# Key and query rows of the first attention stage put in unused weight places, and its transfers in one fixed order

## The chip, the cores and the metric

The kernel runs on one core of one Trainium2 chip. The metric is the device time of one execution in microseconds (us); the quoted time is the median of repeated runs. The engines are TensorE (PE; its weight loads are shown as PEld), VectorE (DVE), ScalarE (ACT), GpSimd (POOL) and SyncE (SP), which here only issues transfers (DMA) between the chip's main memory and its on-chip memory. Each engine works through its instructions in order.

## The reference

Causal attention with a bias that depends on running sums, for 4 batches of 8 heads with 576 tokens and 64 values each, followed by two dense blocks with 2304 tokens, width 512 and inner width 2048.

```python
def _attn_ref(q, k, v, s):
    scores = scale * np.matmul(q, k.transpose(0, 1, 3, 2))
    cum = np.cumsum(np.maximum(s, 0.0), axis=-1)
    bias = -(cum[:, :, :, None] - cum[:, :, None, :])
    scores = np.where(causal, -1000000000.0, scores + np.minimum(bias, 0.0))
    scores = scores - np.max(scores, axis=-1, keepdims=True)
    attn = np.exp(scores)
    attn = attn / (np.sum(attn, axis=-1, keepdims=True) + 1e-09)
    return np.matmul(attn, v)

# x is attn_out with the heads side by side: 2304 x 512
h = x @ w_in
g = np.maximum(h, 0.0) + alpha * np.minimum(h, 0.0)
x = g @ w_out
h = x @ w_in2
y = (h * np.clip(h + 3.0, 0.0, 6.0) / 6.0) @ w_out2
```

The weights arrive as 64-bit floats; the kernel turns them into 32-bit ones on the chip.

## The kernel before

Tokens are taken in two groups for the attention: the first 256 of each batch (stage one), then the other 320. Stage one goes by pairs of heads (`Pair`): batch 0 is pairs 0 to 3, batch 1 pairs 4 to 7, batch 2 pairs 8 to 11. `attention0` first handles pairs 0 to 7, then, in a second call, pairs 8 to 11, while the first dense layer (`moe1`) already runs over the 512 tokens of batches 0 and 1.

One head of a pair passes PE (scores, line 322), DVE (maximum, line 328), ACT (exponential, line 333), DVE (sum and reciprocal, lines 334 and 335), POOL (scaling, line 337), PE (transposition, line 593), ACT or DVE (copy `pT`, lines 595 and 597); the pair's values follow on PE (line 603), ACT (`xhi`, line 611) and DVE (`xlo`, line 612). The running sums of `s` are made once (`cumulate`), written to `cum_scratch` in main memory, and read back as four extra rows beside the keys and queries, two of them data and two constants, so that one matmul adds the bias. Pairs 0 and 1 do without: their biases come from extra matmuls with `pick` and `cum2`. For all others the tile `kr` holds four places (`Rows.n = 4`), and pair i uses place i mod 4. So pair 6 waits for place 2 until pair 2's scores are done, pair 7 for pair 3, and pairs 8 to 11 for pairs 4 to 7. Values (`vraw`, one tile for two pairs) have three buffers.

The weights of the first layer come in 8 units (`load_unit`) of four tiles of 512 KB, each of which has a place of its own in on-chip memory (`wi60`, `wo71` and so on: matrix, unit, part). A unit is read raw, then turned into two 32-bit halves by `split_part`: ACT (lines 142 and 160, sometimes 150), POOL (lines 144 and 147), DVE (lines 152, 155, 161). `moe1` goes through 16 slices f of the inner width, two per unit: 12 matmuls into `h` (line 248), ACT (line 697), DVE with `beta` (line 698), ACT (line 701), DVE (line 702), and 12 matmuls into `y` (line 675), two slices behind. `beta` is made by DVE from `alpha_sb` (line 307), whose transfer is issued in `cumulate`.

A planner in the framework lays out each engine's order of instructions from its own estimate of when each is ready; earlier lines of the program come first among those that are ready, and conversions of weights stand back behind the attention in stage one. Instructions marked `pin` or `keep_in_program_order` stay in the order of the program. All transfers named here are issued by SP. The order on SP before is: `s`, pairs 0 to 3, sums out, rows for pairs 2 to 5, pairs 4 and 5, units 0 and 1, `alpha`; then pair 6 with its rows and pair 7 with its rows when their places are free, units 2 and 3, the keys of pairs 8 to 11 with their rows, units 4 to 7 with the values of pairs 8 to 11 among them.

Of the kernel before, what the change touches and what calls it, by code (L numbers as in the profile page):

```python
# [9 lines left out]
F32 = mybir.dt.float32  # L10
# [5 lines left out]
P = 128  # L16
# [8 lines left out]
WB0 = 6  # L25
WB = 4

W_LD = (9, 11)
W_AT = (5, 11)

A2_AT = 4
# [30 lines left out]
def attention_moe_moe(ctx, tc, qt, kt, kq2, kqs, vs4, vp, s, w_in1, w_out1, alpha, w_in2, w_out2, out):  # L62

    nc = tc.nc
# [217 lines left out]
    def cumulate(pool, pairs):  # L282

        pin = tc.keep_in_program_order
        cum2, pick, zero = pool.cum2, pool.pick, pool.zero
        s_sb = pool.tile([BH, S], F32, tag="wcv", bufs=WB0, name="s_sb")
        pin(nc.sync.dma_start(s_sb, s))
        for pr in pairs[:4]:
            pr.load(pool, pin)
        nc.vector.tensor_scalar(s_sb, s_sb, 0.0, 8.0, op0=ALU.max, op1=ALU.mult)  # L290
        cum = pool.tile([BH, S], F32, tag="wcv", bufs=WB0, name="cum")
        nc.vector.tensor_tensor_scan(cum, s_sb, zero[:BH].to_broadcast([BH, S]), initial=0.0, op0=ALU.add, op1=ALU.add)
        for c0, c1, copies in ((0, NA, 2), (NA, S, 1)):
            cols = slice(c0, c1)
            for j in range(copies):
                high = cum2[j * D : j * D + BH, cols]
                pin(nc.scalar.activation(high, cum[:, cols], AF.Copy))
                pin(nc.vector.tensor_tensor(cum2[j * D + BH : (j + 1) * D, cols], cum[:, cols], cum2[:BH, cols].bitcast(F32), op=ALU.subtract))
            pin(nc.sync.dma_start(cum_d[:, :, cols].rearrange("t b s -> (t b) s"), cum2[:D, cols].bitcast(F32)))
            if c0 == 0:  # L300
                pool.rows.load(2, 2, pin)
                pool.rows.load(4, 2, pin)
        for pr in pairs[4:6]:
            pr.load(pool, pin)
        load_w1(2)
        pin(nc.sync.dma_start(alpha_sb, alpha))
        nc.vector.tensor_scalar(beta, alpha_sb, -1.0, 1.0, op0=ALU.mult, op1=ALU.add)

# [229 lines left out]
    class Rows:  # L538


        n = 4

        def __init__(self, pool):
            self.kq = pool.tile([P, self.n, 2, 2, NA], F32, name="kr")
            keys = self.kq[:R, :, 0].rearrange("r n j k -> r n (j k)")
            nc.scalar.activation(keys, ident[:R, None, :1].to_broadcast([R, self.n, 2 * NA]), AF.Copy, scale=0.0, bias=-1.0)
            nc.gpsimd.memset(self.kq[:R, :, 1], 1.0)

        def load(self, first, n, pin=lambda ins: ins):
            at = first % self.n  # L550
            for which in range(2):
                rows = slice(which * R // 2, (which + 1) * R // 2)
                for j in range(2):
                    src = cum_d[:, 2 * first + j : 2 * (first + n) : 2, :NA]
                    pin(nc.sync.dma_start(self.kq[rows, at : at + n, which, j], src))

    values_of = {}

    class Pair:
# [5 lines left out]
        def load(self, pool, pin=lambda ins: ins):  # L565
            i, self.pool = self.i, pool
            if i < 2:
                kq = pool.tile([P, 2, NA], F32, tag="wcv", bufs=WB0, name="kq")
                self.k, self.q = kq[:, 0], kq[:, 1]
                pin(nc.sync.dma_start(kq, kq2[i]))  # L570
            else:
                kq = pool.rows.kq[:, i % Rows.n]
                self.k, self.q = kq[:, 0], kq[:, 1]
                pin(nc.sync.dma_start(kq[R : R + D], kqs[i - 2]))
            if i % 2 == 0:
                self.load_v(pin)

        def load_v(self, pin=lambda ins: ins):
            i, pool = self.i, self.pool
            values_of[i // 2] = pool.tile([P, 4, 2, D], F32, tag="vraw", bufs=3 if i < H else 2, name="vraw")  # L580
            pin(nc.sync.dma_start(values_of[i // 2], vs4[i // 2]))

        def scores(self, j):
# [30 lines left out]
    def attention0(pool, pairs, lag):  # L614
# [15 lines left out]
        def ahead(to):  # L630
            nonlocal loaded
            while loaded <= min(to, len(pairs) - 1):
                if pairs[0].i == 0:
                    pairs[loaded].load(pool, tc.keep_in_program_order)
                    pool.rows.load(loaded, 1, tc.keep_in_program_order)
                else:
                    pairs[loaded].load(pool)
                loaded += 1

        if pairs[0].i == 0:  # L640
            keep_clock(pool.busy, 18)
            cumulate(pool, pairs)
            loaded = 6
        else:
            pool.rows.load(H, H // 2)
        ahead(1)
        for i, pr in enumerate(pairs):
            for j in range(2):
                waiting.append((pr, j, pr.scores(j)))
                if j == 1:  # L650
                    ahead(i + (Rows.n if pairs[0].i == 0 else 2))
                if len(waiting) > lag:
                    finish()
                yield
# [78 lines left out]
    def attend(att, upto, pool=None):  # L733

        nonlocal done
        while done < upto:
            done += 1
            next(att, None)
            if pool is not None and done in W_LD:
                load_w1(len(units) + 1)  # L740
            if pool is not None and done in W_AT:
                more_w(pool)

# [345 lines left out]
```

## Time and profile before

| what | value |
|---|---|
| median of 3 runs | 1001.95 us (1001.57 to 1003.31) |
| time of the profiled execution | 1001.04 us |
| its span, first to last instruction | 999.3 us, so 1.74 us lie around it |
| mean granted TensorE clock | 0.989 of full speed |
| PE busy | 972.0 us, 97% |
| DVE busy | 614.2 us, 61% |
| ACT busy | 633.0 us, 63% |
| POOL busy | 439.4 us, 44% |

The shares are means over the whole span. The change touches what happens in the first tenth of it, so the table says little on it, and stretches of that tenth have to be read for themselves.

### The profile page before, as it was taken

The page shows a single profiled execution, that of the slowest core. Times are in us where ns is not written, and L with a number is a line of the kernel's source. Part 1 is how long each engine was busy: PE and PEld are TensorE (multiplying, and loading weights), DVE is VectorE, ACT ScalarE, POOL GpSimd, SP SyncE. Part 2 cuts the span into 40 slices and gives each one's busy share as a digit, 9 for nine tenths or more (in the row PEclk, how much of TensorE's full clock was granted, in tenths as well). Part 3 has the DMA queues.
Part 4 walks back from the last instruction along what each step waited for, and adds up shares of the span by engine and source line. Part 5 has one row for each costly group of instructions (what it writes and reads, how often), then busy time and mean ns, then how long its engine had stood idle before and what let it go on. Part 6 is the DMA issues. An engine that isn't in the chain of part 4 may idle for free.

```text
span 999.3 us, 18072 instructions
## 1 busy us (share of the span) xinstructions
PE 972.0 (97%) x6218; PEld 873.5 (87%) x6218; DVE 614.2 (61%) x1502; ACT 633.0 (63%) x1434; POOL 439.4 (44%) x587
## 2 busy tenths in 40 slices
PE   8689999999999999999999999999999999999998
PEld 5468788999999998998998888999999988888886
DVE  6858884466666666666654885977658863222222
ACT  6668778678768778778855655756656743232322
POOL 6554667657666667666643763433112230000000
PEclk9879999999999999999999999999999999999999
DMA  6990014113122223122105322434248734333422
GB/s 220 298 358 1 24 31 132 41 46 91 53 76 74 61 67 98 52 67 83 52 14 177 109 91 72 191 118 144 98 169 304 257 130 151 103 127 91 162 64 85
DMA packets 59828, 114.47 MB, mean 115 GB/s; under 512 B 5704, under 2 KB 21880, under 8 KB 59736
## 3 DMA queue, kind: packets, MB, share of 16 engines
q1 hardware_dynamic: 59736, 113.32, 34.3%
q8 instruction: 49, 0.80, 0.3%
q14 instruction: 43, 0.35, 0.1%
HBM read 84.84 MB, written 28.46 MB: 113 GB/s over the span
## 4 chain that ended last, share of the span: by engine, by line
PE 93%; DMA 2%; ACT 2%; issue 1%; DVE 1%; SPq 0%; POOL 0%; ACTq 0%; DVEq 0%; POOLq 0%
PE y L675 20%; PE h L248 20%; PE o L1042 20%; PE a L879 10%; PE b L879 5%; PE s L410 4%; PE pv L472 4%; PE pt L447 4%; PE c L879 2%; PE s L322 2%; DMA vraw<-in_vs 1%; DMA kr<-cum_scratch 1%; PE h L534 1%; PE pv L603 1%; DMA wraw<-in_w_out 1%
## 5 line engine op out<-in xcount | busy, mean ns | idle before, releaser
L248 PE MATMUL h<-xhi,wi 128*128 128x256 f32 (+1 forms) x896 | 227.0, 322 | 2.8 <-DVE gt L698 1.5
L1042 PE MATMUL o<-wo,gh 128*128 128x512 f32 x576 | 173.5, 389 | 1.1 <-DVE gt L893 1.1
L248 PEld LDWEIGHTS h<-xhi,wi 128*128 128x128 f32 x896 | 156.4, 191 | 16.4 <-DVE gt L698 1.9
L675 PE MATMUL y<-gh,wo 128*128 128x256 f32 (+1 forms) x896 | 162.0, 315 | 0.0
L675 PEld LDWEIGHTS y<-gh,wo 128*128 128x128 f32 x896 | 133.8, 190 | 11.2 <-ACT gh L701 0.4
L248 PE MATMUL h<-xlo,wi 128*128 128x256 f32 (+1 forms) x448 | 143.2, 320 | 0.2 <-DVE xlo L612 0.2
L161 DVE TENSOR_TENSOR gl<-gr,gh 128x512 fp32r<-128x512 f32 (+1 forms) x80 | 51.3, 643 | 126.5 <-ACT gh L160 111.9
L1042 PEld LDWEIGHTS o<-wo,gh 128*128 128x128 f32 x576 | 107.9, 188 | 23.5 <-DVE gt L893 1.3
L160 ACT ACTIVATE gh<-gr 128x512 fp32r<-128x512 f32 (+1 forms) x80 | 46.9, 588 | 119.3 <-PE o L1042 117.7
L879 PE MATMUL a<-x,wc 128*128 128x288 f32 x768 | 112.9, 295 | 0.3 <-ACT z L886 0.3
L144 POOL TENSOR_SCALAR wcv<-wcv 128x512 f32<-128x512 f32 x64 | 47.7, 753 | 142.0 <-ACT wcv L142 139.0
L1042 PE MATMUL o<-wo,gl 128*128 128x512 f32 x288 | 108.2, 389 | 0.0
L879 PEld LDWEIGHTS a<-x,wc 128*128 128x128 f32 x768 | 106.0, 188 | 0.8 <-ACT z L886 0.5
L675 PE MATMUL y<-gl,wo 128*128 128x256 f32 (+1 forms) x448 | 91.6, 317 | 0.0
L248 PEld LDWEIGHTS h<-xlo,wi 128*128 128x128 f32 x448 | 85.6, 191 | 6.5 <-DVE xlo L612 0.7
L422 POOL TENSOR_SCALAR t<-t,rec 128x384 f32<-128x384 f32 (+2 forms) x96 | 65.4, 683 | 57.5 <-DVE rec L421 32.3
L413 DVE CUSTOM_DVE_ANT_0 t<-s,mask 128x384 f32<-128x384 f32 (+2 forms) x96 | 53.4, 563 | 53.3 <-PE pt L447 34.1
L698 DVE SCALAR_TENSOR_TENSOR gt<-gt,beta,h 128x256 f32<-128x256 f32 (+1 forms) x112 | 61.7, 552 | 32.2 <-ACT gt L697 31.0
L418 ACT ACTIVATE t<-t,m 128x384 f32<-128x384 f32 (+2 forms) x96 | 67.1, 700 | 17.0 <-DVE m L413 15.8
L675 PEld LDWEIGHTS y<-gl,wo 128*128 128x128 f32 x448 | 69.7, 190 | 6.0 <-issue 0.2
L702 POOL TENSOR_TENSOR gl<-gt,gh 128x256 fp32r<-128x256 f32 x80 | 59.1, 740 | 29.3 <-ACT gh L701 27.4
L701 ACT ACTIVATE gh<-gt 128x256 fp32r<-128x256 f32 (+1 forms) x112 | 53.1, 476 | 29.3 <-DVE gt L698 27.7
(135 smaller groups left out, 2000.3 us busy)
## 6 DMA issues: line engine op xcount, KB each, us to landing
g_scratch<-gt SPq DMA_DIRECT2D x64, 288.0 KB
wraw<-in_w_in SPq DMA_DIRECT2D x32, 512.0 KB
wraw<-in_w_out SPq DMA_DIRECT2D x32, 512.0 KB
gr<-g_scratch SPq DMA_DIRECT2D x16, 1024.0 KB
kraw<-in_kt SPq DMA_DIRECT2D x32, 288.0 KB
qraw<-in_qt SPq DMA_DIRECT2D x32, 160.0 KB
vraw<-in_vp SPq DMA_DIRECT2D x32, 160.0 KB
y_scratch<-yt SPq DMA_DIRECT2D x18, 256.0 KB
```

What stands on the lines that cost most here:

```text
L144: keep(nc.gpsimd.tensor_scalar(cf, cf, W_MOST, -W_MOST, op0=ALU.min, op1=ALU.max))
L161: keep(nc.vector.tensor_tensor(lo, of, hi.bitcast(F32), op=ALU.subtract))
L248: nc.tensor.matmul(dst, lt, r, start=first and i == 0, stop=last and i == len(terms) - 1)
L413: nc.vector.tensor_tensor_reduce(t[:n, a:e], sc[:n, : e - a], mask[:n, MASK + n - (e - a) :][:, : e - a] if e == w else mask[:n, : e - a], ...
L418: nc.scalar.activation(t[:n, :w], t[:n, :w], AF.Exp, bias=m[-1][:n], scale=-1.0, accum_out=den[:n])
L422: nc.gpsimd.tensor_scalar(t[:n, :w], t[:n, :w], rec[:n], 1.0, op0=ALU.mult, op1=ALU.mult)
L675: nc.tensor.matmul(ys[dc // per][:, o : o + n], which[:, dc * P : (dc + 1) * P], gg, start=(f == 0 and which is wl and dc % per == 0), sto ...
L698: nc.vector.scalar_tensor_tensor(gt, gt, beta[:, f : f + 1], hp[:, :n], op0=ALU.mult, op1=ALU.add)
L701: nc.scalar.activation(gh, gt, AF.Copy)
L702: (nc.vector if n == 512 else nc.gpsimd).tensor_tensor(gl, gt, gh.bitcast(F32), op=ALU.subtract)
L879: nc.tensor.matmul(dst[:, :NX2], lt, r, start=first and n == 0, stop=n == len(terms) - 1, skip_group_check=not first,)
L1042: nc.tensor.matmul(op[i], lt[:, tsl], r, start=(f == 0 and r is wh and lt is gh), stop=(f == FC - 1 and lt is gl))
```

## The change

Pairs 2 to 7 get a tile each. These tiles (`Pair.fill`) lie in places of the weights' units 6 and 7, whose raw weights are now loaded only once the pairs are done. Each is filled with its constants by one ACT instruction and one POOL instruction, and gets its rows by two transfers (`load_rows`). Pairs 8 to 11 have the tile `Rows` for themselves, filled by two POOL instructions, with four transfers of keys and four of rows. Nothing of stage one waits for a place any more. The order on SP is written out in `cumulate`: `s`, pairs 0 to 3, sums out, rows of pairs 2 to 5, pairs 4 and 5, unit 0, pairs 6 and 7 with their rows, unit 1, keys and rows of pairs 8 to 11, units 2 to 5, `alpha`. The values have four buffers in place of three. The loads of units 2 and 3 after steps 9 and 11 of stage one (`W_LD`) go.

```diff
--- before.py
+++ after.py
@@ -25,7 +25,6 @@
 WB0 = 6
 WB = 4
 
-W_LD = (9, 11)
 W_AT = (5, 11)
 
 A2_AT = 4
@@ -285,6 +284,8 @@
         cum2, pick, zero = pool.cum2, pool.pick, pool.zero
         s_sb = pool.tile([BH, S], F32, tag="wcv", bufs=WB0, name="s_sb")
         pin(nc.sync.dma_start(s_sb, s))
+        for pr in pairs[2:]:
+            pr.fill()
         for pr in pairs[:4]:
             pr.load(pool, pin)
         nc.vector.tensor_scalar(s_sb, s_sb, 0.0, 8.0, op0=ALU.max, op1=ALU.mult)
@@ -298,11 +299,17 @@
                 pin(nc.vector.tensor_tensor(cum2[j * D + BH : (j + 1) * D, cols], cum[:, cols], cum2[:BH, cols].bitcast(F32), op=ALU.subtract))
             pin(nc.sync.dma_start(cum_d[:, :, cols].rearrange("t b s -> (t b) s"), cum2[:D, cols].bitcast(F32)))
             if c0 == 0:
-                pool.rows.load(2, 2, pin)
-                pool.rows.load(4, 2, pin)
+                for pr in pairs[2:6]:
+                    pr.load_rows(pin)
         for pr in pairs[4:6]:
             pr.load(pool, pin)
+        load_w1(1)
+        for pr in pairs[6:]:
+            pr.load_rows(pin)
+            pr.load(pool, pin)
         load_w1(2)
+        pool.rows.load(pin)
+        load_w1(NU - 2)
         pin(nc.sync.dma_start(alpha_sb, alpha))
         nc.vector.tensor_scalar(beta, alpha_sb, -1.0, 1.0, op0=ALU.mult, op1=ALU.add)
 
@@ -538,21 +545,18 @@
     class Rows:
 
 
-        n = 4
-
         def __init__(self, pool):
-            self.kq = pool.tile([P, self.n, 2, 2, NA], F32, name="kr")
-            keys = self.kq[:R, :, 0].rearrange("r n j k -> r n (j k)")
-            nc.scalar.activation(keys, ident[:R, None, :1].to_broadcast([R, self.n, 2 * NA]), AF.Copy, scale=0.0, bias=-1.0)
-            nc.gpsimd.memset(self.kq[:R, :, 1], 1.0)
-
-        def load(self, first, n, pin=lambda ins: ins):
-            at = first % self.n
+            self.kq = pool.tile([P, H // 2, 2, 2, NA], F32, name="kr")
+            for which in range(2):
+                nc.gpsimd.memset(self.kq[:R, :, which], 2.0 * which - 1.0)
+
+        def load(self, pin):
+            for i in range(H // 2):
+                pin(nc.sync.dma_start(self.kq[R : R + D, i], kqs[H + i - 2]))
             for which in range(2):
                 rows = slice(which * R // 2, (which + 1) * R // 2)
                 for j in range(2):
-                    src = cum_d[:, 2 * first + j : 2 * (first + n) : 2, :NA]
-                    pin(nc.sync.dma_start(self.kq[rows, at : at + n, which, j], src))
+                    pin(nc.sync.dma_start(self.kq[rows, :, which, j], cum_d[:, 2 * H + j : 3 * H : 2, :NA]))
 
     values_of = {}
 
@@ -566,18 +570,31 @@
             i, self.pool = self.i, pool
             if i < 2:
                 kq = pool.tile([P, 2, NA], F32, tag="wcv", bufs=WB0, name="kq")
-                self.k, self.q = kq[:, 0], kq[:, 1]
                 pin(nc.sync.dma_start(kq, kq2[i]))
+            elif i < H:
+                kq = self.kq
+                pin(nc.sync.dma_start(kq[R : R + D], kqs[i - 2]))
             else:
-                kq = pool.rows.kq[:, i % Rows.n]
-                self.k, self.q = kq[:, 0], kq[:, 1]
-                pin(nc.sync.dma_start(kq[R : R + D], kqs[i - 2]))
+                kq = pool.rows.kq[:, i - H]
+            self.k, self.q = kq[:, 0], kq[:, 1]
             if i % 2 == 0:
                 self.load_v(pin)
 
+        def fill(self):
+            part, nm = divmod(self.i % 4, 2)
+            self.kq = wp.tile([P, 2, 2, NA], F32, tag=f"{('wi', 'wo')[nm]}{NU - 2 + self.i // 4}{part}", name="kr")
+            keys = self.kq[:R, 0].rearrange("r j k -> r (j k)")
+            nc.scalar.activation(keys, ident[:R, :1].to_broadcast([R, 2 * NA]), AF.Copy, scale=0.0, bias=-1.0)
+            nc.gpsimd.memset(self.kq[:R, 1], 1.0)
+
+        def load_rows(self, pin):
+            for which in range(2):
+                rows = slice(which * R // 2, (which + 1) * R // 2)
+                pin(nc.sync.dma_start(self.kq[rows, which], cum_d[:, 2 * self.i : 2 * self.i + 2, :NA]))
+
         def load_v(self, pin=lambda ins: ins):
             i, pool = self.i, self.pool
-            values_of[i // 2] = pool.tile([P, 4, 2, D], F32, tag="vraw", bufs=3 if i < H else 2, name="vraw")
+            values_of[i // 2] = pool.tile([P, 4, 2, D], F32, tag="vraw", bufs=4 if i < H else 2, name="vraw")
             pin(nc.sync.dma_start(values_of[i // 2], vs4[i // 2]))
 
         def scores(self, j):
@@ -630,25 +647,19 @@
         def ahead(to):
             nonlocal loaded
             while loaded <= min(to, len(pairs) - 1):
-                if pairs[0].i == 0:
-                    pairs[loaded].load(pool, tc.keep_in_program_order)
-                    pool.rows.load(loaded, 1, tc.keep_in_program_order)
-                else:
-                    pairs[loaded].load(pool)
+                pairs[loaded].load(pool)
                 loaded += 1
 
         if pairs[0].i == 0:
             keep_clock(pool.busy, 18)
             cumulate(pool, pairs)
-            loaded = 6
-        else:
-            pool.rows.load(H, H // 2)
+            loaded = len(pairs)
         ahead(1)
         for i, pr in enumerate(pairs):
             for j in range(2):
                 waiting.append((pr, j, pr.scores(j)))
                 if j == 1:
-                    ahead(i + (Rows.n if pairs[0].i == 0 else 2))
+                    ahead(i + 2)
                 if len(waiting) > lag:
                     finish()
                 yield
@@ -736,8 +747,6 @@
         while done < upto:
             done += 1
             next(att, None)
-            if pool is not None and done in W_LD:
-                load_w1(len(units) + 1)
             if pool is not None and done in W_AT:
                 more_w(pool)
```

## Rows read from the trace of the kernel before

**Rows 1.** Stretches: length; busy us (instructions) of PE, PEld, DVE, ACT, POOL; PEclk; DMA share; GB/s.

```profile
25.00:69.00 44.00, 31.06 (x161) 20.84 (x162) 32.11 (x110) 27.16 (x79) 23.99 (x43) 0.80 0.98 342
31.88:69.00 37.12, 25.93 (x122) 17.57 (x121) 25.26 (x88) 22.48 (x64) 19.63 (x34) 0.77 0.97 352
55.00:65.00 10.00, 7.08 (x40) 4.86 (x39) 7.80 (x35) 6.86 (x25) 3.94 (x8) 0.99 1.04 409
65.00:72.70 7.70, 7.70 (x28) 5.47 (x27) 5.59 (x20) 6.88 (x20) 6.94 (x13) 0.56 0.97 384
69.00:148.00 79.00, 79.00 (x362) 63.62 (x362) 66.10 (x104) 62.35 (x111) 48.66 (x65) 0.98 0.11 34
```

**Rows 2.** Chain that ended last: start us, us, what it was.

```profile
24.79 9.17 DMA vraw<-in_vs
...
35.97 6.18 DMA wraw<-in_w_out
...
42.16 8.38 DMA kr<-cum_scratch
...
50.68 1.62 PE s L322 x4
...
68.96 6.19 PE h L248 x20
```

**Rows 3.** Timeline of SP, which issues transfers: start, us, line, transfer, count.

```profile
20.34 0.33 SPq L306 DMA_DIRECT2D alpha_sb<-in_alpha  x1
...
24.79 0.33 SPq L581 DMA_DIRECT2D vraw<-in_vs  x1
...
40.96 4.00 SPq L555 DMA_DIRECT2D kr<-cum_scratch  x4
```

**Rows 4.** What SP waited for: us in total, times, longest.

```profile
SPq L555 <- DMA wraw<-in_w_out: 5.4, 4, 2.6
```

**Rows 5.** Timeline of DVE; in brackets the idle time before and its releaser.

```profile
27.16 0.68 DVE L152 SCALAR_TENSOR_TENSOR wcv<-wcv,wraw 128x512 uint32<-128x512 uint32 x1
...
31.88 0.17 DVE L307 TENSOR_SCALAR beta<-alpha_sb 128x16 f32<-128x16 f32 x1
...
35.32 0.29 DVE L328 CUSTOM_DVE_ANT_0 t<-s,mask 128x128 f32<-128x128 f32 x1 [1.88 <-PE s L322]
...
40.56 0.99 DVE L152 SCALAR_TENSOR_TENSOR wcv<-wcv,wraw 128x512 uint32<-128x512 uint32 x1
...
55.91 0.29 DVE L328 CUSTOM_DVE_ANT_0 t<-s,mask 128x128 f32<-128x128 f32 x1 [5.42 <-PE pv L603]
...
64.54 0.66 DVE L161 TENSOR_TENSOR wo<-wcv,wo 128x512 fp32r<-128x512 f32 x1
...
67.25 0.75 DVE L698 SCALAR_TENSOR_TENSOR gt<-gt,beta,h 128x512 f32<-128x512 f32 x1 [0.67 <-ACT gt L697]
```

**Rows 6.** Timeline of ACT: the first fill and the first unit's conversion.

```profile
2.02 1.91 ACT L546 ACTIVATE kr<-ident 4x2048 f32<-4x2048 f32 x1
...
20.35 0.67 ACT L142 ACTIVATE wcv<-wraw 128x512 f32<-128x512 f32 x1 [1.86 <-DMA wraw<-in_w_in]
```

**Rows 7.** Timeline of PE: the run of matmuls before the first scores.

```profile
1.45 7.00 PE L534 MATMUL h<-busy 128*128 128x512 bf16 x18 [1.45 <-DVE busy L757]
```

**Rows 8.** Timeline of POOL.

```profile
1.73 1.79 POOL L547 MEMSET kr<- 4x2048 f32 x1
...
3.96 3.48 POOL L763 TENSOR_SCALAR pick<-ident 32x32 fp32r<-32x32 f32 x8
11.83 0.83 POOL L337 TENSOR_SCALAR t<-t,rec 128x128 f32<-128x128 f32 x2 [4.39 <-DVE rec L335]
...
40.99 2.21 POOL L337 TENSOR_SCALAR t<-t,rec 128x128 f32<-128x128 f32 x2
```

**Rows 9.** Timeline of DVE: second half of unit 2 converted.

```profile
81.84 0.68 DVE L161 TENSOR_TENSOR wi<-wcv,wi 128x512 fp32r<-128x512 f32 x1
```

**Rows 10.** Timeline of PE: the matmuls that read it.

```profile
85.89 0.48 PE L248 MATMUL h<-xhi,wi 128*128 128x512 f32 x1
```

## The prediction

> **What bounds the kernel now.** I read the windows of the first 150 us, then the chain of waits through the slow part of them, then SP's timeline, to see why transfers come late, then those of DVE, ACT and POOL, to see what would be late next.
>
> The windows show where time lies open. From 69 us to 148 us PE is busy in all 79.00 us [rows 1]: whatever is gained must be gained ahead of that, and reaches the end only if PE then stays as full. In the 44 us from 25 to 69 PE is busy for 31.06 us, DVE for 32.11, ACT for 27.16 and POOL for 23.99. So PE is idle for 12.9 us and DVE for 11.9 us, and DVE is the busiest.
>
> The chain of waits says on what [rows 2]. From 24.79 to 50.68 us it runs almost wholly through transfers: the values of pair 6 (9.17 us), a tile of weights (6.18 us), the rows of pair 8 (8.38 us). Only then do the scores of pair 8 go, and at 68.96 us PE's full stretch begins with slice 2 of the first layer. The reader is to see that small loads stand in one queue with 512 KB tiles. SP gives the values of pair 6 out at 24.79 us, after `alpha` at 20.34 us and so behind all eight tiles of units 0 and 1; the rows of pair 8 go out from 40.96 us, behind units 2 and 3 [rows 3]. For the rows alone SP waited 5.4 us on earlier tiles of weights [rows 4].
>
> What does a late transfer cost? Read on DVE, which carries most work here: its timeline has two waits that end with a pair whose data were late [rows 5]. One of 1.88 us ends at 35.32 us, when pair 6's scores come. One of 5.42 us ends at 55.91 us: DVE starts on pair 8, whose buffers lie where those of pairs 0 to 7 lay and come free with pair 7's values, and those stood on PE behind pair 8's scores, which waited for the rows. Together 7.3 us. The other 4.6 us of DVE's 11.9 are short waits of the chain PE, DVE, ACT, POOL.
>
> **The change, part by part.** *Order of transfers.* Unit 0 keeps its place, and its first tile lands by 20.35 us, when ACT ends a wait for it [rows 6]. With 409 GB/s, the rate of a stretch full of weights [rows 1], a tile of 512 KB takes 1.28 us and a load of 256 KB 0.64. So I estimate: unit 0 in by 20.35 + 3 x 1.28 = 24.2; pairs 6 and 7 (three loads of 256 KB and four small ones) by about 26.5; unit 1 by 31.6; pairs 8 to 11 by 34.5; units 2 to 5 (16 tiles, 20.5 us) by 55; `alpha` by about 55.5. So pair 6 can be scored some 8 us before DVE's wait at 35.32 ended, pair 8 some 16 us before 50.68. Unit 1 comes some 5 us later by it, but it is converted behind unit 0: before, the conversion of these two units on DVE runs from 27.16 to 65.2 us [rows 5], so that costs nothing. With the data there, both waits of DVE go: **-7.3 us**. The bounds: -1.9 us if only the first of them goes, -11.9 us if all of DVE's idle time in the stretch is filled.
>
> *Fills.* ACT has six instructions of 4x512 for one of 4x2048, which took 1.91 us [rows 6]. Between a quarter of that each (no change in sum) and 0.67 us each, as for the 128x512 conversion beside it, that is 0 to 2.1 us more, at a time when PE runs its opening matmuls from 1.45 to 8.45 us [rows 7]; PE can't score before 8.45, which covers it. POOL has two of 4x2048 and six of 4x512 for one that took 1.79 us [rows 8]: by the same quarter, 2 x 1.79 + 6 x 0.45 = 6.3, so 4.5 us more. `pick`, 3.48 us from 3.96 on, is needed for the first scores; it is earlier in the program, and POOL's next work after it is at 11.83 us, so 4.4 us of idle time wait there. But the transfers of rows need the fills. I take **+0.5 us**, between 0 and +4.5 (all of it ahead of `pick`).
>
> *Row transfers.* 16 small ones in place of 20; with nobody waiting at their end: 0.
>
> *`alpha` last.* `beta` is first used at 67.25 us before [rows 5]. With the gain that is about 61 us, against 55.5 for the transfer: hidden, by some 5 us.
>
> *Weights.* Units 4 and 5 come earlier, 6 and 7 wait for pairs 6 and 7, long done by 55 us: 0. The fourth buffer of values: 0, as no row shows anything waiting for one alone.
>
> *Denser work.* The two engines disturb each other: DVE's step on line 152 took 0.68 us at 27.16 and 0.99 us at 40.56 [rows 5], and beside it two scalings on POOL took 2.21 us at 40.99, against 0.83 at 11.83 [rows 8]. Less idle time brings more of that: I take **+0.5 us**, from 0 to +3 (24 conversion steps on DVE in the stretch, first at 27.16, last at 64.54, a third of them slowed by 0.3 us on both engines).
>
> If the two excluded each other strictly, those 24 steps of 0.68 us (16.3) and POOL's 23.99 us would take 40.3 of the 44 us already: a rival, below. I don't take it for the sum, because POOL's 23.99 holds the time in which it was blocked.
>
> The Trainium skill ("SBUF — State Buffer", the section on the doors to the memory) says that a GpSimd instruction and a VectorE one with two inputs from that memory share a pair of ports as an exclusive lock, held for a whole instruction. By it the gain would stop at the rival's size; the trace agrees in kind, by the 2.21 against 0.83 us.
>
> *Clock.* From 65 to 72.7 us the granted clock is 0.56, so most of it at 1.2 GHz, while PE is busy throughout [rows 1]. At 2.4 GHz those 7.7 us would take 7.7 x 0.56 = 4.3: 3.4 us to gain, if PE is fuller before. The engines ahead of it decide, and the same mix of work comes before it: 0, with -3.4 as its bound.
>
> Sum: -7.3 + 0.5 + 0.5 = **-6.3 us**. Against the profiled execution, 999.3 + 1.74 around it = 1001.04 us, that gives 994.7. The runs' median lies 0.9 us above that execution, so I say **995.0 us**. A difference under about 0.2% (2 us) can't be told from none here.
>
> **Rivals.** *All open time is filled.* Pairs 6 to 11 in time let PE, DVE and POOL mesh: DVE's 11.9 us and the clock's 3.4 go: 15.3, about 986 us. For it speaks that no engine is busy for more than 32.11 of the 44 us; against it, that a head goes through four engines in turn, so that short waits stay. Chance 0.12.
>
> *Conversion decides.* PE's full stretch takes weights as they come: unit 2's second half is done on DVE at 81.84 + 0.68 = 82.5 us [rows 9], and the matmuls that read it start at 85.89 us [rows 10], only 3.4 us behind. If conversion, with DVE at 66.10 of 79 us, can't move up, PE waits at slice 4, and the gain is at most 3.4 us: 997.6 to 1001, middle 999. Against it: conversion of unit 1's end and unit 2 stood behind pair 8 on POOL and DVE before, and so moves with it. Chance 0.12.
>
> *DVE and POOL exclude each other.* Then the stretch can shrink from 44 to 40.3 us, by 3.7, whatever comes early: 997.3 us. For it, the stretched steps above; against it, the blocked time that is counted twice. Chance 0.06. (The rule named above says this.)
>
> *Slower: `beta` blocks DVE.* `beta` stands at 31.88 us in DVE's order [rows 5]. If the planner expects `alpha` early and leaves `beta` there, DVE stands until 55.5 us with 25.26 us of work [rows 1] behind it: it reaches the state of 69 us at 80.8, 11.8 us later, 1013 us. It decides from the point at which over 13.5 us (69 - 55.5) of that work stands behind `beta`. Against it: before, `beta` came only when `alpha` was surely there, since DVE did not idle ahead of it. Chance 0.10.
>
> **How the numbers follow.** The forecast has 0.60, with a range of its own of 991 to 998.5 from the bounds of its terms. The range runs from 988.5 to 1000.8: it leaves out most of the first rival, 0.09, all of the last, 0.10, and the edge of the conversion case, 0.01. Faster by over 0.2%: 0.60 x 0.97 + 0.12 + 0.12 x 0.35 + 0.06 x 0.8 = 0.79; slower 0.10 + 0.01 = 0.11; the rest, 0.10, is no change.
>
> **What would show it.** Right: scores of pair 6 by 27 us and of pair 8 before 48; no wait of DVE over 2 us between 30 and 60 us; the chain of waits without transfers of `vraw` and `kr` after 30 us; PE's full stretch from about 62 us and 79 us without a gap after it. Wrong: a long wait of DVE that ends with `beta`; PE waiting for `wi` around slice 4; the first scores well after 8.4 us; a second stretch at 1.2 GHz longer than 7.7 us.

## The result, and where the time went

The changed kernel takes 1010.23 us (median of 6 runs, 1008.96 to 1012.14); the kernel before takes 1002.8 us beside it. The ratio is 1.0073, with an interval of 1.0054 to 1.0091. It is slower, by some 7 us, where 995.0 us was predicted, and it lies outside the range. The profiled execution took 1009.54 us, with a span of 1007.7 us; all times below are in it.

Start where the change acts first. POOL's timeline of the changed kernel, and under it the first scores on PE (start, us, line, what, count, and in brackets the idle time before and what ended it):

```profile
1.73 3.85 POOL L551 MEMSET kr<- 4x2048 f32 x2
5.53 1.91 POOL L588 MEMSET kr<- 4x512 f32 x4
...
7.63 0.98 POOL L588 MEMSET kr<- 4x512 f32 x2
8.59 1.77 POOL L772 TENSOR_SCALAR pick<-ident 32x32 fp32r<-32x32 f32 x8
```

```profile
9.31 0.32 PE L329 MATMUL s<-cum,pick 64*128 64x128 f32 x1 [1.05 <-POOL pick L772]
```

All fills stand ahead of `pick`, which starts at 8.59 us where it started at 3.96 [rows 8]. PE, which was busy with its opening matmuls until 8.45 us [rows 7], now waits 1.05 us for it. That is about one microsecond. The next lines show what stood late behind it: ACT's timeline, and then DVE's.

```profile
21.67 0.66 ACT L141 ACTIVATE wcv<-wraw 128x512 f32<-128x512 f32 x1 [2.87 <-DMA wraw<-in_w_in]
23.03 0.66 ACT L141 ACTIVATE wcv<-wraw 128x512 f32<-128x512 f32 x1 [0.70 <-DMA wraw<-in_w_out]
```

```profile
24.97 0.19 DVE L341 TENSOR_SCALAR den<-den 128x2 f32<-128x2 f32 x1 [4.21 <-ACT t L340]
...
57.19 0.28 DVE L335 CUSTOM_DVE_ANT_0 t<-s,mask 128x128 f32<-128x128 f32 x1
...
63.17 0.57 DVE L314 TENSOR_SCALAR beta<-alpha_sb 128x16 f32<-128x16 f32 x1 [1.08 <-DMA alpha_sb<-in_alpha]
...
70.01 0.76 DVE L160 TENSOR_TENSOR wo<-wcv,wo 128x512 fp32r<-128x512 f32 x1
...
72.70 0.75 DVE L709 SCALAR_TENSOR_TENSOR gt<-gt,beta,h 128x512 f32<-128x512 f32 x1 [1.22 <-ACT gt L708]
```

The first tile of unit 0 is awaited until 21.67 us, 1.3 us later than before [rows 6], and ACT stands for it with heads behind it in its order; DVE stands 4.21 us for those. It is natural to put the late tile down to the fills, but SP's waits (us in total, times, longest) speak against it, first of the kernel before, then of the changed one:

```profile
SPq L555 <- DMA cum_scratch<-cum: 2.5, 1, 2.5
```

```profile
SPq L593 <- DMA cum_scratch<-cum: 3.7, 1, 3.7
```

SP issues unit 0 behind the rows of pairs 2 to 5, and these wait until the sums written to `cum_scratch` have landed, 2.5 us before and 3.7 now. So the first tile goes out 1.3 us later. The lines are SP's, of the kernel before, of the changed one, and of e1 and e8 below:

```profile
14.24 0.59 SPq L127 DMA_DIRECT2D wraw<-in_w_in  x1
```

```profile
15.51 0.59 SPq L126 DMA_DIRECT2D wraw<-in_w_in  x1
```

```profile
15.27 0.59 SPq L126 DMA_DIRECT2D wraw<-in_w_in  x1
```

```profile
14.43 0.59 SPq L127 DMA_DIRECT2D wraw<-in_w_in  x1
```

With `pick` ahead of the fills (e1) the tile goes out 1.0 us late as well, and with the fills ahead of `pick` in the kernel before (e8) it is only 0.2 us late. So, by these profiles of one execution each, the fills did not make this transfer late. What made the sums land later is not shown; in e10, whose edit touches only later steps, the rows went out at 10.02 us in place of 10.52.

The waits for pair 6 (1.88 us) and ahead of pair 8 (5.42 us) are gone, as predicted, but both pairs come later: pair 6 to DVE at 37.92 us, against 35.32 before, and pair 8 at 57.19, against 55.91 [rows 5]. The last step of unit 1's conversion, the end of the row of conversion steps, is at 70.01 us (64.54 before), and the first `gt` of the first layer 2.7 us behind it, as before (67.25 against 64.54): 5.45 us late.

The chain that ended last (start, us, what) shows the queue:

```profile
1.80 3.78 POOL kr L551 x2
...
17.12 9.81 DMA wraw<-in_w_out
...
30.71 10.69 DMA kr<-in_kqs
...
44.49 9.58 DMA wraw<-in_w_in
54.09 9.05 DMA alpha_sb<-in_alpha
...
73.50 5.43 PE h L247 x12
```

`vraw` and the cumulated rows have left it, but the keys of pairs 8 to 11 are in it at 30.71 us, where I had said that no `kr` would be, and transfers still fill it from 17 to 63 us, each of 9 to 11 us from its issue. The fills are in it too, in the place of PE's opening matmuls. PE's slice 2 starts at 73.50 us instead of 68.96 [rows 2].

Two of the stretches of [rows 1], and the 25 us ahead of them:

```profile
0.00:25.00 25.00, 18.80 (x98) 11.56 (x99) 10.99 (x47) 13.63 (x39) 15.49 (x39) 0.98 0.68 199
25.00:69.00 44.00, 36.09 (x177) 24.58 (x176) 34.18 (x126) 27.46 (x90) 23.30 (x44) 0.81 0.99 349
69.00:148.00 79.00, 77.82 (x348) 61.35 (x347) 64.13 (x105) 65.75 (x115) 52.06 (x68) 0.94 0.10 33
```

From 25 to 69 us PE and DVE are busier than before by 5.03 and 2.07 us: the stretch is denser, but it began with more left to do: up to 25 us DVE had been busy for 10.99 us, where it was busy for 15.46 before, and PE for 18.80 in place of 22.31. In the 79 us that were full, PE is idle for 1.18 us and the clock is at 0.94 instead of 0.98. By these two rows the clock alone takes 0.04 x 79, an estimate of some 3 us of PE's time, so it is a good part of the loss.

How much of the loss is there by the end of the first layer's blocks? SP's stores of their results, first before and then after:

```profile
161.36 0.85 SPq L686 DMA_DIRECT2D y_scratch<-yt  x2
...
225.97 0.90 SPq L686 DMA_DIRECT2D y_scratch<-yt  x2
```

```profile
166.34 0.38 SPq L697 DMA_DIRECT2D y_scratch<-yt  x1
...
233.43 0.39 SPq L697 DMA_DIRECT2D y_scratch<-yt  x1
```

5.0 us at the first block, 7.5 at the second, 8.4 in the span: more than half of it is there at the first block, and most of the rest at the second.

### The profile page after: what moved, and what is told of

It reads as the page before. It is cut to its first block, busy times and chain, and to the rows that moved or that the text cites. A ratio compares the mean times of both kernels' runs of the same rounds, so it can differ in the third digit from the quotient of the medians.

```text
span 1007.7 us, 18107 instructions
## 1 busy us (share of the span) xinstructions
PE 980.6 (97%) x6218; PEld 879.4 (87%) x6218; DVE 616.9 (61%) x1502; ACT 635.9 (63%) x1439; POOL 446.3 (44%) x594
## 4 chain that ended last, share of the span: by engine, by line
PE 88%; DMA 4%; ACT 3%; DVE 1%; SPq 1%; POOL 1%; issue 1%; ACTq 0%; DVEq 0%; POOLq 0%
PE o L1051 19%; PE y L686 19%; PE h L247 19%; PE a L888 10%; PE b L888 5%; PE s L417 4%; PE pv L479 4%; PE pt L454 4%; PE c L888 2%; DMA kr<-in_kqs 1%; DMA wraw<-in_w_out 1%; DMA wraw<-in_w_in 1%; DMA alpha_sb<-in_alpha 1%; PE s L329 1%; SPq L126 1%
## 5 line engine op out<-in xcount | busy, mean ns | idle before, releaser
L143 POOL TENSOR_SCALAR wcv<-wcv 128x512 f32<-128x512 f32 x64 | 50.7, 801 | 134.4 <-ACT wcv L141 130.6
```

The lines of the kernel that those rows point to most:

```text
L143: keep(nc.gpsimd.tensor_scalar(cf, cf, W_MOST, -W_MOST, op0=ALU.min, op1=ALU.max))
```

## The experiments

The theories at the start: A, the fills ahead of `pick` cost the start; B, `alpha` comes late; C, earlier heads of pairs 6 and 7 push the conversion of units 0 and 1 back; D, only the planner's new order. Ratios are to the kernel before, with their intervals; "first `gt`" is line 709's (698 in the kernel before) on DVE.

**e1_pick_first.** `pick` and the memsets pinned in the order in which they are written, `pick` first.

```
-    nc.gpsimd.memset(self.kq[:R, 1], 1.0)
+    tc.keep_in_program_order(nc.gpsimd.memset(self.kq[:R, 1], 1.0))
...   (the same for Rows' memsets and for pick)
```

> The changed kernel with its constant fills on POOL put behind the eight instructions that make pick. Late start (theory A: the fills ahead of pick make the first scores 0.9 us late, and the units' transfers 1.3 us late, and ACT then stands on unit 0 while heads wait): first scores back at 8.4 us, ACT's wait for unit 0 below 2 us, time down by 3 to 5 us from the changed kernel, to about 1006. Late alpha (theory B): down by at most 1 us. Early heads push the conversion of weights back (theory C): down by at most 1.5 us. Re-planning as such (theory D): a change of either sign up to 3 us.

1004.82 us, 1.0016 (1.0002 to 1.003): 0.0057 of the 0.0073 is back. The heads come early now (first scores at 7.54 us), but look at DVE's timeline:

```profile
50.90 0.29 DVE L335 CUSTOM_DVE_ANT_0 t<-s,mask 128x128 f32<-128x128 f32 x1
...
64.40 0.17 DVE L314 TENSOR_SCALAR beta<-alpha_sb 128x16 f32<-128x16 f32 x1 [3.08 <-DMA alpha_sb<-in_alpha]
...
67.96 0.85 DVE L160 TENSOR_TENSOR wo<-wcv,wo 128x512 fp32r<-128x512 f32 x1
...
70.05 0.74 DVE L709 SCALAR_TENSOR_TENSOR gt<-gt,beta,h 128x512 f32<-128x512 f32 x1
```

Pair 8 is 5.0 us earlier than before, as the forecast wanted; yet DVE then waits 3.08 us for `alpha`, unit 1's conversion ends 3.4 us later than before, and the first `gt` is 2.8 us late.

**e2_alpha_early.** The transfer of `alpha` right behind that of `s`.

```
         pin(nc.sync.dma_start(s_sb, s))
+        pin(nc.sync.dma_start(alpha_sb, alpha))
...
         load_w1(NU - 2)
-        pin(nc.sync.dma_start(alpha_sb, alpha))
```

> The changed kernel with alpha transferred right after s. Theory B (beta and so the first layer's gate wait for alpha at 63 us): DVE's beta before 20 us, the first gate before 68 us in place of 72, time down by 3 to 5 us. Theory A and C: at most 1 us down. Theory D: up to 3 us of either sign.

1007.28 us, 1.0043 (1.0028 to 1.0058). About 3 us back, just clear of noise; first `gt` at 71.45.

**e3_pick_alpha.** Both edits.

> Both edits, pick ahead of the fills and alpha right after s. If A and B each hold part of the loss, the two gains add: down by 6 to 9 us, to the time of the kernel before or below. Theory C: down by at most 2 us.

1005.24 us, 1.0021 (1.0009 to 1.0033): no better than e1 alone. `beta` no longer stops DVE and the first `gt` is at 68.31, still later than before. The two gains don't add.

**e4_unit1_first.** Unit 1's transfers ahead of pairs 6 and 7.

```
-        load_w1(1)
+        load_w1(2)
         for pr in pairs[6:]:
...
-        load_w1(2)
```

> The changed kernel with unit 1 of the weights transferred ahead of pairs 6 and 7, as before the change. Theory C (pairs 6 and 7 early take DVE and ACT from the conversion of units 0 and 1, which then runs at 49 to 60 us in place of 41 to 50): conversion of unit 1's first half moves up by 4 us or more and the time goes down by 3 to 6 us. Theory A and B: within 1 us of the changed kernel, or slower.

1008.48 us, 1.0061 (1.0042 to 1.008), first `gt` at 72.18. With the late start left in, unit 1's place in the queue does nothing that is clear of noise, which speaks against theory C. The run shows something else too: ACT waited only 0.27 and 0.62 us for unit 0 here (its line stands with e10), and nearly all of the loss stayed.

**e5_free_conversion.** The first step of each conversion was pinned in the first stage. That holds it to the written order of heads and transfers: in all six profiles so far the conversions went in three rounds, at about 20, 33 to 40 and 50 to 58 us. The pin goes.

```
-            first = tc.keep_in_program_order if bufs == WB0 else keep
+            first = keep
```

> The changed kernel with one edit: the conversion of units 0 and 1 in the first stage is no longer bound to the written order of the heads. Theory G (the first slice of the first layer goes about 2.1 us after unit 1's last conversion step, in all six profiles so far, so early heads that push unit 1's conversion back cost time): the last conversion step of unit 1 comes earlier than 70.0 us, the first relu of the first layer earlier than 72.1 us by about as much, and most of what it comes earlier is kept at the end: 1003 to 1007 us. Rival (the late start by the fills alone, theory A): nothing that the start set is touched, 1009 to 1011 us. Rival D (the seven us are only another order found by the planner): no clear relation between the first relu and the end.

1006.79 us, 1.0026 (1.0011 to 1.0041). First `gt` at 65.78, 6.9 us earlier; the loss falls from 0.0073 to 0.0026, by 4.7 us.

**e6_pick_alpha_free.** The edits of e1, e2 and e5.

> The changed kernel with three edits: pick ahead of the fills, alpha transferred right behind s, and the conversion of units 0 and 1 free of the written order of the heads. Theory G: pick first and alpha first together gave 1005.24 us and a first relu at 68.31 us, conversion then being what is left; with it free the first relu comes before 66.6 us (that of the kernel before) and the time below 1002 us. Rival (the early start is all there is to have back): 1004 to 1006 us.

1001.70 us, 0.9978 (0.9965 to 0.9992): just faster than before. First `gt` at 59.69, 7.56 us earlier than before.

**e7_before_free.** The kernel before with the edit of e5.

> The kernel before with the conversion of units 0 and 1 free of the written order of the heads. Theory G: its first relu (66.64 us) stood 2.1 us behind unit 1's last conversion step (64.54 us), and DVE waited 5.4 us for the last four heads' rows before it, so the conversion can move up into that wait: first relu 1 to 4 us earlier and 999 to 1002 us. Rival (conversion follows what DVE has to do and the order doesn't matter): 1002 to 1004 us.

1005.72 us, 1.0023 (1.0009 to 1.0038): slower, though its first `gt` comes at 63.70, 3.55 us earlier. A miss for "earlier conversion is better". From 69 to 148 us PE is busy for 76.45 us there, against 79.00 before.

**e8_before_fills.** The kernel before, with the extra fills alone, into a tile that nothing reads, pinned ahead of `pick`.

```
+        spare = wp.tile([P, CH, 2], F32, tag="wi50", name="spare")
+        for n in (CH, CH, CH // 2, CH // 2, CH // 2, CH // 2, CH // 2, CH // 2):
+            tc.keep_in_program_order(nc.gpsimd.memset(spare[:4, :n], 1.0))
```

> The kernel before with the changed kernel's extra fills alone: eight memsets on POOL (two of 4x1024 and six of 4x512, into a tile that nothing reads) ahead of pick. Theory A (the start is lost to the fills and the loss is kept): the first scores go from 8.38 us to 9.3 or later, the transfers of the cumulated rows about 1 us later, and the time is 1005 to 1009 us, as taking the fills from ahead of pick gave back 5.4 us in the changed kernel. Theory C (the order of transfers is the cause, the start costs what it is late): 1003 to 1004.5 us.

1009.38 us, 1.005 (1.0034 to 1.0065): the fills alone make the kernel before some 5 us slower. PE's timeline, DVE's, and ACT's:

```profile
9.89 0.32 PE L322 MATMUL s<-cum,pick 64*128 64x128 f32 x1 [2.04 <-POOL pick L766]
```

```profile
30.20 0.17 DVE L307 TENSOR_SCALAR beta<-alpha_sb 128x16 f32<-128x16 f32 x1 [4.21 <-DMA alpha_sb<-in_alpha]
...
76.15 0.75 DVE L698 SCALAR_TENSOR_TENSOR gt<-gt,beta,h 128x512 f32<-128x512 f32 x1
```

```profile
21.56 1.22 ACT L142 ACTIVATE wcv<-wraw 128x512 f32<-128x512 f32 x2
```

A start 1.5 us late is 8.9 us at the first `gt`. How it grew is not what the changed kernel shows: ACT doesn't wait for unit 0 at all, and DVE stands 4.21 us for `alpha` with `beta` next in its order, which it did not before [rows 5]. The edit also did more than delay `pick`: DVE's step on `s_sb`, from which the running sums are made, took 2.12 us in place of 1.18, and the sums came 0.9 us late.

**e9_before_pick.** The kernel before with `pick` pinned ahead of the memset of `kr`.

> The kernel before with pick pinned ahead of POOL's memset of kr, so that its first scores start at 7 to 7.7 us as in the changed kernel with pick first. With the three kernels measured (before, before with the fills ahead of pick, the changed kernel with and without them ahead) it fills the table of start by order of transfers. If the start alone carried the loss of the changed kernel, this one and the changed kernel with pick first (1004.82 us) are the same within 1.5 us, 1003 to 1005. If the new order of transfers costs by itself, this one is faster than 1002 us. Rival (an earlier start gives nothing back, the places of heads and conversion in each engine's order decide): 1003 to 1006 us, with the first store of the first layer later than 161 us.

1003.36 us, 0.9994 (0.9975 to 1.0013): the same, though the first scores come at 7.29 us instead of 8.38. ACT's timeline, then DVE's:

```profile
21.32 0.66 ACT L142 ACTIVATE wcv<-wraw 128x512 f32<-128x512 f32 x1 [3.25 <-DMA wraw<-in_w_in]
```

```profile
38.66 0.29 DVE L328 CUSTOM_DVE_ANT_0 t<-s,mask 128x128 f32<-128x128 f32 x1 [2.29 <-PE s L322]
```

ACT waits longer at unit 0's conversion (3.25 us, 1.86 before [rows 6]), about as much as the heads had gained, and pair 6 comes later than before [rows 5]. With e1, e8 and the changed kernel this fills a table of ratios:

| | `pick` first | as written before | fills ahead of `pick` |
|---|---|---|---|
| transfers of before | 0.9994 (e9) | 1 | 1.005 (e8) |
| transfers of the change | 1.0016 (e1) | | 1.0073 |

The columns differ by 0.0056 and 0.0057, the rows by 0.0022 and 0.0023; by the intervals of its two runs, each difference is good to some 0.0024 either way. So within that the two parts of the loss add up, and the fills' place is the larger, some 5.6 us. The other 2.3 us, for all the rest of the change, would not be clear of noise in one row alone.

**e10_unit0_later.** The changed kernel, fills and all, with unit 0's conversion written two heads later: `W_AT = (7, 11)` in place of `(5, 11)`.

> The changed kernel with the conversion of unit 0 written two heads later (W_AT 7 and 11), the fills left ahead of pick. Theory H (the one microsecond of the start grew to five because ACT, in its written order, stood at unit 0's conversion until unit 0's transfers had landed, 2.87 and 0.70 us, with ready heads behind it): ACT no longer waits there for a transfer, the heads of pairs 2 to 5 come 3 to 4 us earlier than in the changed kernel, and the time is 1004 to 1007 us. Rival (the conversion ends the stage, so that putting it later makes things worse): first relu later than 72.1 us and 1010 to 1014 us.

1007.84 us, 1.0024 (1.0006 to 1.0041). The median is above what theory H gave (1007), the ratio is within it: beside this run the kernel before took 1004.05. ACT's timeline has the two steps without a wait:

```profile
23.79 1.22 ACT L141 ACTIVATE wcv<-wraw 128x512 f32<-128x512 f32 x2
```

First `gt` at 69.67 us, 3.0 earlier than in the changed kernel; 0.0049 of the 0.0073 (0.0025 either way) is recovered with the late start left in place. So the place of unit 0's conversion in ACT's order is worth about as much as the fills cost. That the fills' cost passed through ACT's wait for unit 0 does not follow. ACT's first step of unit 0 in e4 and in e5:

```profile
20.51 0.68 ACT L141 ACTIVATE wcv<-wraw 128x512 f32<-128x512 f32 x1 [0.27 <-DMA wraw<-in_w_in]
```

```profile
21.13 0.67 ACT L141 ACTIVATE wcv<-wraw 128x512 f32<-128x512 f32 x1 [4.21 <-DMA wraw<-in_w_in]
```

e4 hardly waits and is at 1.0061, e5 waits longest and is at 1.0026, e8 doesn't wait and is at 1.005. And of what theory H said, only a part came: DVE reaches pairs 4 and 5 at 25.70 and 27.75 us, 3.4 and 6.1 earlier than in the changed kernel, but pairs 2 and 3 later, and the first block of the first layer is stored no earlier (167.19 us against 166.34). What carried the fills' cost stays open.

**e11_free_unit1_first.** The edits of e1, e2, e4 and e5 together.

> Pick first, alpha early, conversion free of the written order (1001.7 us) and unit 1 transferred ahead of pairs 6 and 7. If unit 1's late arrival still holds its conversion back, the first relu comes before 59 us and the time is 998 to 1001 us. If after the first relu it is unit 2 (transferred behind all of the rows) and the stretch of PE at its limit that decide, 1000 to 1003 us.

999.28 us, 0.9957 (0.9938 to 0.9976): the fastest, and faster than both kernels. DVE's timeline and two windows:

```profile
53.25 0.28 DVE L334 CUSTOM_DVE_ANT_0 t<-s,mask 128x128 f32<-128x128 f32 x1
...
54.14 0.68 DVE L160 TENSOR_TENSOR wo<-wcv,wo 128x512 fp32r<-128x512 f32 x1
...
58.05 0.75 DVE L708 SCALAR_TENSOR_TENSOR gt<-gt,beta,h 128x512 f32<-128x512 f32 x1 [0.78 <-ACT gt L707]
```

```profile
25.00:69.00 44.00, 35.16 (x169) 25.52 (x170) 37.32 (x107) 29.67 (x82) 30.55 (x45) 0.88 1.01 361
...
69.00:148.00 79.00, 78.38 (x368) 61.59 (x367) 64.55 (x105) 59.48 (x108) 44.41 (x57) 1.00 0.04 14
```

In the slow stretch DVE is idle for 6.7 us, where it was idle for 11.9. Pair 8 comes at 53.25 and the last step of unit 1 is at 54.14, 10.4 us earlier than before. Against e6 the gain is 0.0021, good to 0.0023 either way.

**e12_before_all_free.** Is this the change's doing, or that of the three small edits? The kernel before, with `pick` first, `alpha` early and the conversion free, but with its own places and transfers of pairs 2 to 11.

> The kernel before with the same three small edits as the fastest kernel so far (pick first, alpha early, conversion free of the written order), but the old places and transfers of pairs 2 to 11, units 1 and 2 each behind them as before. If the change's places for pairs 6 to 11 are worth what the two waits of DVE for them were (the prediction's 7.3 us, of which the fastest kernel shows some), this one stays at 1002 us or above and the fastest kernel (999.28) is some 4 to 7 us better than it. If those places bring nothing and the three edits bring all, it comes to 998 to 1001 us too.

1007.32 us, 1.0031 (1.0016 to 1.0045). The same three edits that the changed kernel needs make the old one slower. Its chain of waits, and its timeline of DVE (the profiled execution, 1010.13 us, is the longest of its 12):

```profile
42.67 8.70 DMA kr<-cum_scratch
```

```profile
59.58 0.29 DVE L328 CUSTOM_DVE_ANT_0 t<-s,mask 128x128 f32<-128x128 f32 x1 [0.86 <-PE pv L603]
...
64.22 0.72 DVE L698 SCALAR_TENSOR_TENSOR gt<-gt,beta,h 128x512 f32<-128x512 f32 x1
```

The rows of pair 8 are the last to come again (as in [rows 2]), pair 8 is 6.3 us later than in e11, and so is the first `gt`, by 6.2 us. With the same three edits, the new places and order (unit 1 first) give 0.9957 against 1.0031, so 0.0074 or some 7.4 us; without unit 1 first (e6) 5.3; each is good to some 2 us either way. That is against a kernel which the edits had made 3.1 us slower: against the kernel before as it stands, e11 gains 0.0043, or 4.3 us. A kernel that holds the change is the fastest, but only with the rest fitted to it.

**All runs beside one landmark.** First `gt` on DVE, and ratio:

| conversion in written order | first `gt`, us | ratio | conversion free | first `gt`, us | ratio |
|---|---|---|---|---|---|
| e9 | 66.53 | 0.9994 | e11 | 58.05 | 0.9957 |
| before | 67.25 | 1 | e6 | 59.69 | 0.9978 |
| e3 | 68.31 | 1.0021 | e7 | 63.70 | 1.0023 |
| e10 | 69.67 | 1.0024 | e12 | 64.22 | 1.0031 |
| e1 | 70.05 | 1.0016 | e5 | 65.78 | 1.0026 |
| e2 | 71.45 | 1.0043 | | | |
| e4 | 72.18 | 1.0061 | | | |
| changed | 72.70 | 1.0073 | | | |
| e8 | 76.15 | 1.005 | | | |

Within a family the end follows the landmark by about one thousandth (1 us) for each us, with e8 as the exception. The families lie apart: 63.70 us with free conversion is no better than 68.31 or 69.67 in written order. What lies between is lost behind the landmark. Take SP's stores of the first layer's results, of which the kernel before starts the first at 161.36 us, the fifth at 225.97, the ninth at 373.76 and the thirteenth at 532.38. e7 starts the first at 160.62 and the fifth at 230.85, 4.9 us behind. e5 is ahead up to the fifth (160.60, 224.82) and 3.4 us behind at the ninth (377.13). e11 is 9.0 us ahead at the first (152.41), but at the thirteenth (529.89) only 2.5. How full PE is from 69 to 148 us doesn't tell the families apart (e1 78.27 us, e3 78.28; e6 77.92, e11 78.38), and its clock there is higher with free conversion (1.00, against 0.92 to 0.98). Which of the later work costs it is not shown. So theory D has its share: a new order of later work takes up to some 5 us in these runs, and a landmark of the first stage alone does not tell the end.

## Why the prediction was wrong

*Late transfers, -7.3 us.* This is the step that failed most: that DVE's two waits, once gone, would come off the time. From the forecast (995.0 of 1001.95 us, 0.9931) to the result (1.0073) it is some 14 us, and 8 to 9 of them lie here: with `pick` ahead of the fills (e1) the change still takes 1.6 us more, or 2.3 by the table of e9, where the sum without its fills was -6.8. The waits went, the small loads left the chain, and with the start restored pair 8 came at 50.90 us (e1). But the waits had something else's time in them: unit 1's conversion must be done before the first layer runs, and it stands in the same orders. In e1 it ended 3.4 us later than before, and the first `gt` came 2.8 us late. With that conversion freed, e6 has 0.0043 less than e3, and with unit 1 first as well, e11 is faster than before by 4.3 us. Against an old kernel with the same edits the places are worth 5.3 to 7.4 us (e6, e11 against e12). That lies near 7.3, but it is measured against a kernel that those edits had slowed by 3.1 us, so it does not bear the size out.

*Fills, +0.5 us, bounds 0 to +4.5.* The second step that failed, by some 5 of the 14 us, in its size and its reason. "`pick` is earlier in the program" says nothing of where the planner puts it: the fills had no bound to `pick`, and it put all of them ahead. The durations were right (6.3 us estimated; 3.85 + 1.91 + 0.98 = 6.74 measured). The price was above even the upper bound: some 5.6 us by the table of e9, for a start 0.9 us (changed kernel) and 1.5 us (e8) later. I had costed POOL's time and let its idle time and PE's opening matmuls cover most of it. Why a microsecond at the start became five at the end is not settled: in the changed kernel ACT stood for unit 0, whose transfer the fills had not delayed, and in e8 DVE stood for `alpha`.

*Sum and range.* 994.7 and 0.9 make 995.6, not 995.0. And the forecast's own range, 991 to 998.5, does not come from the bounds of its terms, as it says: added up they reach from 985.7 to 1006.6 us. The measured time is above even these.

*Landings.* I had divided bytes by 409 GB/s from the moment of unit 0. But SP's queue holds an issue back: pair 7's load went out at 25.41 us and the last four pairs' row transfers took SP from 31.35 to 37.10, so the weights started late. `alpha` landed at 63.1 us (54.09 + 9.05) instead of 55.5.

```profile
25.41 0.52 SPq L576 DMA_DIRECT2D kr<-in_kqs  x1
26.95 0.40 SPq L126 DMA_DIRECT2D wraw<-in_w_in  x1
...
31.35 5.75 SPq L559 DMA_DIRECT2D kr<-cum_scratch  x4
...
54.09 0.33 SPq L313 DMA_DIRECT2D alpha_sb<-in_alpha  x1
```

(SP's timeline of the changed kernel.) "Hidden, by some 5 us" was thus wrong: DVE waited 1.08 us for it as it is, and 3.08 once the heads were early.

*Row transfers, 0.* In all they take SP less than before (10.6 us against 13.9), but the 5.75 us in the fence above now stand ahead of sixteen tiles of weights and `alpha`. What that costs the end was not tried by itself.

*Unit 1 later "costs nothing".* Its transfers alone cost nothing clear of noise with the late start (e4: 1.0061 against 1.0073), and with the rest free 0.0021 (e6 to e11), at the edge of noise. But I had taken the first `gt` for an end that pair 8 sets: with the conversion in written order it goes with unit 1's last step, 2.1 to 3.4 us behind it in all nine such kernels, whatever pair 8 does (e1).

*Clock, 0.* Not so either. I had allowed for a gain alone, and the clock went the other way: from 69 to 148 us it is at 0.94 against 0.98, some 3 us of PE's time by the estimate above. In e11 it is 1.00 there, so that what stood as a bound can be had. What it takes is not shown: in the 44 us ahead of that stretch PE was busy for 35.16 us in e11 and for 36.09 in the changed kernel.

*Rivals.* "Slower: `beta` blocks DVE" had the sign and a wrong mechanism: the planner did move `beta` behind nearly all the work, to 63.17 us, and its wait cost 1.08 us. "Conversion decides" was right that, in written order, conversion sets when the first layer starts, but wrong in the place: it is unit 1, at the first slice, not unit 2 at slice 4. "DVE and POOL exclude each other" would not have made it slower; no run here is clearly below its 997.3 us, so it stays open.

*What would show it.* Of the signs of a right forecast one came: no wait of DVE over 2 us between 30 and 60 us. Of the signs of a wrong one, the first scores came after 8.4 us (9.31), and the second stretch at 1.2 GHz was longer than 7.7 us: a mean of 0.94 over 79 us has some 9.5 us of it by itself. The wait that ends with `beta` came, but at 1.08 us it was not long.

## What to carry to other kernels

An instruction that is early in the text is early on its engine only if something binds it there: before costing a fill at nothing, ask what else on that engine the first critical result needs, and pin that. A start that is late by 0.9 or 1.5 us cost some 5 us at the end here, so do not cost it one for one; and before a long wait behind it is put down to it, check in another run whether what was awaited was late for that reason. When a stall is removed, look for what else had its time in it: here three edits that together made the old kernel slower were what made the change pay.

## What was not expected of the hardware

A transfer's time from issue to landing here is that of the queue, not of its bytes: `alpha`, 8 KB, took 9.05 us behind tiles of weights, where a 512 KB tile took 9.58 us. And the same eight `pick` instructions on POOL took 3.48 us at 3.96 us in the kernel before [rows 8], and 1.77 us at 8.59 in the changed one. What differed beside them is in the windows of these two moments, first before, then after (length, then PE, PEld, DVE, ACT, POOL):

```profile
3.96:7.44 3.48, 3.48 (x10) 1.26 (x9) 2.67 (x4) 1.30 (x3) 3.26 (x9) 1.00 0.96 290
```

```profile
8.59:10.36 1.77, 1.04 (x8) 1.05 (x9) 0.00 (x0) 0.00 (x0) 1.55 (x9) 1.00 0.14 38
```

DVE was busy for 2.67 of 3.48 us beside the longer ones and not at all beside the shorter. The memsets are not so: four took 1.91 us, 0.48 each, from 5.53 us, and two took 0.98, 0.49 each, from 7.63 us on, in POOL's timeline above, though DVE had steps of its own in the first moment (its timeline in the changed kernel, below) and none in the second. The Trainium skill ("SBUF — State Buffer", section "SBUF: two separate sides") says that a VectorE instruction with two inputs from that memory takes a shared pair of ports against a GpSimd instruction that reads it; a memset reads nothing there. The trace agrees, by these four numbers. ACT and the transfers were busier beside the longer ones too, so the rows alone don't rule those out. DVE's step on `s_sb`, with one input, was long beside memsets: it took 0.45 us in e1, where `pick` stood ahead of them, 1.18 in the kernel before and 2.12 in e8, and in these two it ended 0.3 us behind the end of POOL's memset of `kr` (3.52 and 4.42 us). No run tried that by itself.

```profile
5.77 1.41 DVE L299 TENSOR_TENSOR cum<-cum,cum 32x256 fp32r<-32x256 f32 x3 [0.48 <-ACT cum L298]
```
